# Identity products between the first loads, a new order table, and final sums shared between VectorE and GpSimd in a two-layer state-space and convolution kernel

## The chip, the cores and the metric

One core of one Trainium2 chip. The metric is the device time of one execution in microseconds; lower is better. Times are medians of several runs, with lowest and highest. All runs of this case are in the ordinary ("fast") state.

## The reference, cut to what matters

```python
x = x + A(layernorm(x), ...)   # state recurrence over 2048 steps, 640 channels, complex B, C, Lambda
x = x + B(layernorm(x), ...)   # long convolution by FFT: kv = shift(k) * v; y = irfft(rfft(kv) * rfft(ssm_k)); q * y
x = x + A(layernorm(x), ...)
x = x + B(layernorm(x), ...)   # same weights in both rounds; output bfloat16, 1 x 2048 x 640
```

B's convolution does not depend on `x`, so the kernel makes all of it (transforms as products with cosine and sine tables) in the first part, beside the loads, and only multiplies by it later. The last step, called B2 below, is `out = x + layernorm(x) * Y`, where Y is B's factor.

## The kernel before

Every piece of work is a task with a list of engines, an estimated length and the buffers it uses. A small list scheduler in the kernel's source places all tasks at build time; a table `WHEN` gives each task its rank. The instructions are then emitted in the order of the planned starts, and on the chip each engine takes its own in that order. So a number in `WHEN` decides who stands behind whom, on every engine.

```python
WHEN = {"warm": ..., "yt_ph0": ..., "kv_mm0:0": ..., "a_p0": ..., ...}     # cut: one rank for each task

def e_warm(_):                                   # first thing on TensorE: 72 products of the identity, to raise the clock
    for i in range(72):
        nc.tensor.matmul(s_warm.get()[:, P*(i%4):P*(i%4+1)], lhsT=ident_bf, rhs=ident_bf, start=True, stop=True)

# k-v product of one block: TensorE into one of four PSUM buffers, VectorE empties it (kv_ev)
def e_ev(_, h=h, s_pk=s_pk, s_vT=s_vT):
    nc.vector.tensor_tensor(s_vT.get()[:, sl], s_pk.get()[:], s_vT.get()[:, sl], ALU.mult)

def b_chunk(...):                                # B2: chunks 0 to 2 in one group of 4 quarters, chunk 3 in 4 groups of one
    for qs in groups:
        ... # statistics of the rows, cut
        if len(qs) == 1:                         # each quarter of chunk 3: two fused VectorE instructions
            scalar_tensor_tensor(b, x, nmean, Y, add, mult)          # e_u
            scalar_tensor_tensor(Y, b, rstd, x, mult, add)           # e_m
        else:                                    # whole chunk: normalise on ScalarE or VectorE, one product, four sums
            ln_apply(...)                                            # e_u, 4 times
            nc.vector.tensor_tensor(b, b, Y, ALU.mult)               # e_mm, 2560 columns
            nc.vector.tensor_tensor(Y, b, x, ALU.add)                # e_m, 4 times
```

Of the kernel before, what the change touches and what calls it, by code (L numbers as in the profile page):

```python
# [17 lines left out]
P = 128  # L18
# [34 lines left out]
    "warm": -5, "yt_io0": 2.55, "yt_ph0": 4.27, "yt_sin0": 5.89, "yt_neg0": 9.88, "yt_io6": 132.6, "yt_ph6": 8.2, "yt_sin6": 9.91, "yt_neg6": 13.01,  # L53
    "yt_io12": 8.8, "yt_ph12": 11.54, "yt_sin12": 13.59, "yt_neg12": 16.53, "yt_Ci": 21.14, "yt_Si": 22.8, "yt_nsi": 30.27, "yt_f0": 1.22, "yt_f2": 6.07,
    "yt_f3": 8.4, "yt_f4": 9.65, "yt_h0": 0.07, "yt_h1": 0.97, "yt_h2": 5.13, "yt_h3": 9.63, "kv_dsl": 1.97, "kv_kd": 2.73, "kv_k0": 13.36, "kv_k1":
    14.32, "kv_k2": 14.97, "kv_d0": 5.67, "kv_d1": 6.57, "kv_d2": 10.23, "kv_ds0": 10.65, "kv_lk0": -0, "kv_lv0": 9.8, "kv_mm0:0": 12.25, "kv_ev0:0":
    15.4, "kv_mm0:1": 15.02, "kv_ev0:1": 17.2, "kv_st0": 21.1, "kv_ds1": 13.44, "kv_lk1": 12.55, "kv_lv1": 15, "kv_mm1:0": 21.79, "kv_ev1:0": 25.02,
    "kv_mm1:1": 20.06, "kv_ev1:1": 22.17, "kv_st1": 32.7, "kv_ds2": 18.01, "kv_lk2": 35.6, "kv_lv2": 40.3, "kv_mm2:0": 48.16, "kv_ev2:0": 52.03,
    "kv_mm2:1": 40.92, "kv_ev2:1": 50.79, "kv_st2": 54.8, "kv_ds3": 30.92, "kv_lk3": 47.3, "kv_lv3": 43.8, "kv_mm3:0": 54.17, "kv_ev3:0": 56.25,
    "kv_mm3:1": 57.88, "kv_ev3:1": 59.99, "kv_st3": 76.1, "kv_ds4": 55.32, "kv_lk4": 68.7, "kv_lv4": 72.6, "kv_mm4:0": 78.97, "kv_ev4:0": 81.57,  # L60
    "kv_mm4:1": 72.36, "kv_ev4:1": 77.61, "kv_st4": 85.5, "a_pl": 0.17, "a_p0": 11.24, "a_p1": 13.98, "a_p2": 14.63, "a_p3": 15.78, "a_p4": 18.43, "a_p5":
    20.56, "a_p6": 23.36, "a_lamd": 23.86, "a_f": 28.37, "a_dd": 16.07, "a_ldB0": 2.4, "a_ldB1": 7.4, "a_wl00:0": 34.4, "a_wl00:1": 31.5, "a_wc00:0":
    37.93, "a_wm00:0": 39.1, "a_wc00:1": 40.53, "a_wm00:1": 40.04, "a_wl01:0": 40.21, "a_wl01:1": 37.9, "a_wc01:0": 42.58, "a_wm01:0": 49.98, "a_wc01:1":
    51.1, "a_wm01:1": 53.25, "a_wl02:0": 46.1, "a_wl02:1": 42.6, "a_wc02:0": 48.69, "a_wm02:0": 54.03, "a_wc02:1": 55.37, "a_wm02:1": 58.88, "a_wl03:0":
    71.4, "a_wl03:1": 56.5, "a_wc03:0": 74.94, "a_wm03:0": 75.97, "a_wc03:1": 76.97, "a_wm03:1": 79.87, "a_wl04:0": 65.2, "a_wl04:1": 74.9, "a_wc04:0":
    78.59, "a_wm04:0": 80.65, "a_wc04:1": 81.65, "a_wm04:1": 82.89, "a_b00:0": 9.82, "a_b0e0:0": (10.51, 0), "a_b00:1": 8.06, "a_b0e0:1": (9.33, 3),
    "a_b00:2": 11.53, "a_b0e0:2": (13.01, 1.5), "a_b00:3": 10.63, "a_b0e0:3": (12.42, -1), "a_b00:4": 7.7, "a_b0e0:4": (8.75, 3), "a_b01:0": 49.89,
    "a_b0e1:0": (50.52, 3), "a_b01:1": 14.62, "a_b0e1:1": (17.28, 0.8), "a_b01:2": 23.8, "a_b0e1:2": (24.94, 3), "a_b01:3": 18.33, "a_b0e1:3": (19.59,
    -1), "a_b01:4": 23.52, "a_b0e1:4": (24.36, 1.5), "a_b10:0": 33.92, "a_b1e0:0": (35, 3), "a_b10:1": 32.55, "a_b1e0:1": (33.68, 0), "a_b10:2": 25.31,
    "a_b1e0:2": (26.42, -1), "a_b10:3": 29.77, "a_b1e0:3": (31.02, 0), "a_b10:4": 26.8, "a_b1e0:4": (28.17, 3), "a_b11:0": 42.65, "a_b1e1:0": (43.58, -1),  # L70
    "a_b11:1": 28.31, "a_b1e1:1": (29.65, -1), "a_b11:2": 34.63, "a_b1e1:2": (35.54, -1), "a_b11:3": 46.77, "a_b1e1:3": (48.11, 99), "a_b11:4": 30.56,
    "a_b1e1:4": (31.47, -1), "a_gm0": 84.5, "a_ge0": (87.86, -1), "a_gm1": 87.84, "a_ge1": 90.96, "a_gm2": 104.18, "a_ge2": (107.4, 0), "a_gm3": 98.47,
    "a_ge3": (115.43, 1.5), "a_gm4": 92.78, "a_ge4": 96.07, "a_wl10:0": 97.9, "a_wl10:1": 89.8, "a_wc10:0": 115.48, "a_wm10:0": 107.45, "a_wc10:1":
    111.58, "a_wm10:1": 112.92, "a_wl11:0": 101.84, "a_wl11:1": 103.04, "a_wc11:0": 106.68, "a_wm11:0": 109.36, "a_wc11:1": 121.12, "a_wm11:1": 122.95,
    "a_wl12:0": 116.24, "a_wl12:1": 117.44, "a_wc12:0": 121.91, "a_wm12:0": 132.45, "a_wc12:1": 135.94, "a_wm12:1": 138.06, "a_wl13:0": 131.59,
    "a_wl13:1": 130.39, "a_wc13:0": 137.56, "a_wm13:0": 138.85, "a_wc13:1": 139.99, "a_wm13:1": 141.05, "a_wl14:0": 144.12, "a_wl14:1": 142.92,
    "a_wc14:0": 148.92, "a_wm14:0": 150.68, "a_wc14:1": 153.82, "a_wm14:1": 157.45, "a_ti": 20.17, "a_ta": 22.96, "a_t0": 26.17, "a_t1": 122.82, "a_t2":
    131.25, "yq0_kl": 4.8, "yq0_ka": 15.17, "yq0_KA:m0": 16.75, "yq0_KA:e0": (18.76, -1), "yq0_KA:m1": 19.31, "yq0_KA:e1": 20.32, "yq0_KA:m2": 17.03,
    "yq0_KA:e2": (17.86, -1), "yq0_KA:m3": 18.61, "yq0_KA:e3": (19.66, 99), "yq0_KB:m0": 25.89, "yq0_KB:e0": (27.01, 99), "yq0_KB:m1": 27.38, "yq0_KB:e1":
    (28.75, 0.8), "yq0_KB:m2": 24.08, "yq0_KB:e2": (25.52, 1.5), "yq0_KB:m3": 28.87, "yq0_KB:e3": (30.31, 0), "yq0_KB:m4": 26.57, "yq0_KB:e4": 27.91,  # L80
    "yq0_vl": 26.3, "yq0_VA:m0": 31.92, "yq0_VA:e0": (32.55, 0), "yq0_VA:m1": 31.61, "yq0_VA:e1": (32.24, 6), "yq0_VA:m2": 32.27, "yq0_VA:e2": (33.15,
    0.8), "yq0_VA:m3": 33.47, "yq0_VA:e3": (34.1, 99), "yq0_VB:m0": 35.91, "yq0_VB:e0": 36.98, "yq0_VB:m1": 37.48, "yq0_VB:e1": (38.73, 99), "yq0_VB:m2":
    36.58, "yq0_VB:e2": (37.97, 0), "yq0_VB:m3": 38.79, "yq0_VB:e3": (41.58, 0), "yq0_VB:m4": 40.18, "yq0_VB:e4": (39.51, 1.5), "yq1_kl": 28.99, "yq1_ka":
    34.59, "yq1_KA:m0": 39.9, "yq1_KA:e0": (41.76, 1.5), "yq1_KA:m1": 35.29, "yq1_KA:e1": (35.98, 6), "yq1_KA:m2": 35.57, "yq1_KA:e2": 36.58, "yq1_KA:m3":
    38.6, "yq1_KA:e3": (39.71, 0.8), "yq1_KB:m0": 43.29, "yq1_KB:e0": (44.32, 3), "yq1_KB:m1": 45.76, "yq1_KB:e1": (47.02, 0), "yq1_KB:m2": 44.86,
    "yq1_KB:e2": 46.12, "yq1_KB:m3": 43.97, "yq1_KB:e3": 45.22, "yq1_KB:m4": 47.51, "yq1_KB:e4": 49.78, "yq0_pw": 42.46, "yq0_IB:m0": 52.34, "yq0_IB:e0":
    53.78, "yq0_IB:m1": 51.44, "yq0_IB:e1": (52.78, 99), "yq0_IB:m2": 50.27, "yq0_IB:e2": (51.82, 0), "yq0_IB:m3": 53.95, "yq0_IB:e3": (54.47, 3),
    "yq0_IB:m4": 53.05, "yq0_IB:e4": 54.88, "yq0_tt": 64.47, "yq1_vl": 49.69, "yq1_VA:m0": 56, "yq1_VA:e0": (56.63, -1), "yq1_VA:m1": 57.69, "yq1_VA:e1":
    (58.43, 3), "yq1_VA:m2": 56.43, "yq1_VA:e2": (57.53, 3), "yq1_VA:m3": 56.75, "yq1_VA:e3": (57.6, -1), "yq1_VB:m0": 59.7, "yq1_VB:e0": 60.79,
    "yq1_VB:m1": 61.49, "yq1_VB:e1": (62.75, 0.8), "yq1_VB:m2": 60.37, "yq1_VB:e2": (61.69, 0.8), "yq1_VB:m3": 62.39, "yq1_VB:e3": 63.65, "yq1_VB:m4":  # L90
    61.27, "yq1_VB:e4": (62.15, -1), "yq0_IA:m0": 65.54, "yq0_IA:e0": (66.37, 6), "yq0_IA:m1": 66.03, "yq0_IA:e1": (67.27, 0.8), "yq0_st": 69.05,
    "yq2_kl": 52.2, "yq2_ka": 58.65, "yq2_KA:m0": 64.22, "yq2_KA:e0": (65.38, -1), "yq2_KA:m1": 63.55, "yq2_KA:e1": (64.19, -1), "yq2_KA:m2": 64.8,
    "yq2_KA:e2": (65.43, -1), "yq2_KA:m3": 63.86, "yq2_KA:e3": (64.49, 6), "yq2_KB:m0": 68.05, "yq2_KB:e0": (69.33, 99), "yq2_KB:m1": 66.86, "yq2_KB:e1":
    (68.17, 1.5), "yq2_KB:m2": 68.73, "yq2_KB:e2": (70.23, 0.8), "yq2_KB:m3": 69.62, "yq2_KB:e3": (71.13, 1.5), "yq2_KB:m4": 67.83, "yq2_KB:e4": (69.07,
    1.5), "yq1_pw": 66.59, "yq1_IB:m0": 78.02, "yq1_IB:e0": (79.4, -1), "yq1_IB:m1": 74.47, "yq1_IB:e1": (75.77, 0), "yq1_IB:m2": 76.21, "yq1_IB:e2":
    (77.78, 0.8), "yq1_IB:m3": 77.12, "yq1_IB:e3": (78.82, -1), "yq1_IB:m4": 75.54, "yq1_IB:e4": (76.67, 3), "yq1_tt": 80.49, "yq2_vl": 64.11,
    "yq2_VA:m0": 74.09, "yq2_VA:e0": (74.72, 0), "yq2_VA:m1": 71.61, "yq2_VA:e1": 72.94, "yq2_VA:m2": 71.25, "yq2_VA:e2": (73.84, 3), "yq2_VA:m3": 70.96,
# [278 lines left out]
def c_tt(n, slow=False):  # L376
    return 0.065 + 0.00104 * n if slow else 0.1 + 0.00053 * n
# [500 lines left out]
def b_chunk(S, nc, R, small, c, lname, s_x, sums_in, x_ready, s_Y, y_ready, sums_out, out, groups):  # L878
# [11 lines left out]
    for qs in groups:  # L890
# [4 lines left out]
        for i, q in enumerate(qs):  # L895
# [11 lines left out]
            else:  # L907
# [6 lines left out]
                def e_mm(_):  # L914
                    b = s_b.get()
                    nc.vector.tensor_tensor(b, b, s_Y.get(), ALU.mult)
# [626 lines left out]
```

## Time and profile before

| | before |
|---|---|
| time, median of 3 runs | 358.36 us (358.2 to 359.07) |
| span of the profiled run | 356.8 us |
| TensorE's last product ends | 345.70 us |
| VectorE's last instruction ends | 353.60 us, 7.90 us later |
| intervals of half clock (from the throttle records, before the end) | one, 36.85 to 40.26 us |

Read it as two numbers that add up: where TensorE ends, and how long VectorE still works after that (called the tail below). Some 3 us of store and program end follow.

### The profile page before, as it was taken

To read this page: it belongs to the slowest core of one execution; us is meant where nothing else is said; L and a number is where in the kernel's file an instruction comes from. 1 tells how busy PE (TensorE), PEld (TensorE's weight loads), DVE (VectorE), ACT (ScalarE), POOL (GpSimd) and SP (SyncE) were. 2 spreads that over 40 slices of the span, in tenths; PEclk is the share of its full clock that TensorE was granted. 3 is DMA by queue.
4 is the path that set the end of the run, shared out by engine and by line. 5 is a ranking of instruction groups with operands and counts; after the bars stand their busy time and mean duration, and the time that the engine had idled before them with its cause. 6 is when DMAs were issued, how large, how long until landed. Compare 5 with 4: busy or idle time off the path is not lost.

```text
span 356.8 us, 8409 instructions
## 1 busy us (share of the span) xinstructions
PE 327.5 (92%) x3534; PEld 247.6 (69%) x3565; DVE 315.1 (88%) x479; ACT 256.4 (72%) x406; POOL 20.8 (6%) x51
## 2 busy tenths in 40 slices
PE   7686998989998997999999999999999999999970
PEld 7346876867686986986685677686866767755640
DVE  8799798798799797999999969979999679999896
ACT  3999798898799999943378599797256577306850
POOL 5841003000000000000000000000000000000000
PEclk9999899999999999999999999999999999999996
DMA  7999999999999982790226690605032022220141
GB/s 193 208 235 188 182 184 217 193 186 202 237 245 163 184 174 46 144 233 2 62 73 119 137 333 34 147 18 132 0 68 81 3 16 59 75 75 2 50 172 73
DMA packets 118712, 45.91 MB, mean 129 GB/s; under 512 B 111629, under 2 KB 112914, under 8 KB 118674
## 3 DMA queue, kind: packets, MB, share of 16 engines
q1 hardware_dynamic: 118528, 45.36, 59.9%
q8 instruction: 28, 0.46, 0.5%
q14 instruction: 10, 0.08, 0.1%
q10 hardware_dynamic: 146, 0.01, 0.0%
HBM read 17.38 MB, written 7.86 MB: 71 GB/s over the span
## 4 chain that ended last, share of the span: by engine, by line
PE 69%; ACT 10%; DVE 8%; DMA 7%; issue 3%; SPq 2%; DVEq 0%; ACTq 0%
PE ps L859 31%; PE ps L770 11%; PE ps L773 11%; ACT b L382 6%; PE ps L608 3%; PE ps L1163 3%; DMA b<-in_A_C_im_dram 2%; DMA b<-in_B_v_dram 2%; DVE b L1169 2%; PE ps L1313 2%; DMA b<-b 2%; PE ps L1314 1%; PE ps L1208 1%; SPq L536 1%; DMA b<-in_B_k_dram 1%
## 5 line engine op out<-in xcount | busy, mean ns | idle before, releaser
L382 ACT ACTIVATE b<-ps 128x1024 bf16<-128x1024 f32 (+3 forms) x125 | 109.6, 945 | 29.5 <-PE ps L773 25.5
L859 PEld LDWEIGHTS <-b 128*128 128x128 bf16 x880 | 67.7, 98 | 48.3
L859 PE MATMUL ps<-W,b 128*128 128x128 bf16 (+1 forms) x629 | 95.7, 298 | 0.6
L770 PE MATMUL ps<-b,BT 128*128 128x256 bf16 x400 | 56.8, 273 | 0.0
L773 PE MATMUL ps<-b,BT 128*128 128x256 bf16 x400 | 56.7, 273 | 0.0
L808 DVE TENSOR_TENSOR_SCAN b<-rtab,b 128x1290 bf16<-128x1290 f32 x16 | 44.7, 2833 | 0.3
L773 PEld LDWEIGHTS <-BT 128*128 128x128 bf16 x400 | 39.1, 98 | 4.5
L770 PEld LDWEIGHTS <-BT 128*128 128x128 bf16 x400 | 38.6, 98 | 4.4
L726 ACT ACTIVATE b<-b,nmr,rstd 128x640 bf16<-128x640 f32 (+1 forms) x43 | 37.0, 915 | 6.2 <-DVE nmr L693 6.2
L681 ACT ACTIVATE junk<-b,nmean 128x640 bf16<-128x640 f32 x48 | 39.7, 828 | 1.5
L1232 PE MATMUL ps<-b,b 128*128 128x128 bf16 x170 | 35.1, 219 | 1.2 <-ACT G L382 0.7
L1235 PE MATMUL ps<-b,b 128*128 128x128 bf16 x170 | 35.4, 219 | 0.0
L1237 PE MATMUL ps<-b,b 128*128 128x128 bf16 x150 | 32.8, 219 | 0.0
L1234 PE MATMUL ps<-b,b 128*128 128x128 bf16 x150 | 32.8, 219 | 0.0
L384 DVE CAST b<-ps 128x1024 bf16<-128x1024 f32 (+2 forms) x24 | 26.2, 1109 | 6.3 <-PE ps L1208 2.7
L867 ACT ACTIVATE b<-ps 128x640 f32<-128x640 f32 x16 | 11.1, 697 | 22.8 <-PE ps L859 22.8
L859 PE MATMUL ps<-G,b 128*128 128x128 bf16 (+1 forms) x152 | 26.5, 295 | 0.4
L1163 PE MATMUL ps<-b,fd 128*128 128x512 bf16 x73 | 18.6, 380 | 3.8 <-POOL fd L1141 2.0
L1313 PE MATMUL ps<-b,b 128*128 128x128 bf16 x160 | 19.4, 219 | 2.6 <-ACT b L382 2.1
L1314 PE MATMUL ps<-b,b 128*128 128x128 bf16 x160 | 19.2, 219 | 0.0
L552 ACT ACTIVATE b<-b,s_F 128x640 f32<-128x640 bf16 x20 | 17.2, 859 | 1.8 <-DVE W L556 1.4
L556 DVE SCALAR_TENSOR_TENSOR W<-b,s_F 128x640 bf16<-128x640 bf16 x20 | 17.4, 882 | 1.0 <-ACT b L552 0.7
(210 smaller groups left out, 560.3 us busy)
## 6 DMA issues: line engine op xcount, KB each, us to landing
b<-in_A_x_dram SPq DMA_DIRECT2D x8, 640.0 KB, 4.9
b<-ysd SPq DMA_DIRECT2D x8, 640.0 KB, 5.1
b<-in_B_ssm_k_dram SPq DMA_DIRECT2D x5, 512.0 KB, 8.6
kvd<-b SPq DMA_DIRECT2D x5, 512.0 KB, 4.3
b<-kvd SPq DMA_DIRECT2D x5, 512.0 KB, 5.4
ysd<-b SPq DMA_DIRECT2D x5, 512.0 KB, 5.0
out_dram<-b SPq DMA_DIRECT2D x8, 320.0 KB, 2.2
tab<-in_A_B_re_dram SPq DMA_DIRECT2D x1, 800.0 KB, 7.4
```

The lines of the kernel that those rows point to most:

```text
L382: nc.scalar.activation(out, in_, ACT.Copy)
L681: nc.scalar.activation(small.junk, src(q), ACT.Square, bias=st["nmean"][:, i:i + 1], scale=1.0, accum_out=st["ssq"][:, i:i + 1])
L726: nc.scalar.activation(dst, src, ACT.Identity, bias=st["nmr"][:, i:i + 1], scale=st["rstd"][:, i:i + 1])
L770: nc.tensor.matmul(pb[:, jj, c2, :], lhsT=aw["BT1"][:, c2, j, k, :], rhs=uT[:, 0:2, k, :], start=(k == 0), stop=False)
L773: nc.tensor.matmul(pb[:, jj, c2, :], lhsT=aw["BT0"][:, c2, k, j * P:(j + 1) * P], rhs=uT[:, 2:4, k, :], start=False, stop=(k == NJ - 1))
L808: nc.vector.tensor_tensor_scan(gv, rt, gv, 0.0, ALU.mult, ALU.add)
L859: nc.tensor.matmul(pc[:, o0:o1], lhsT=lh, rhs=rh, start=(n == 0), stop=(n == len(ops) - 1))
L1163: nc.tensor.matmul(pk[:, 512 * b:512 * (b + 1)], lhsT=s_ds.get()[:, l, :], rhs=kT[:, t0:t0 + 512], start=(l == 0), stop=(l == 3))
L1232: nc.tensor.matmul(ps[:, g, 0, :], lhsT=T["Cf"].get()[:, q, :], rhs=are, start=True, stop=single)
L1234: nc.tensor.matmul(ps[:, g, 0, :], lhsT=T["Sf"].get()[:, q, :], rhs=A[:, 2 * q + 1, :], start=False, stop=True)
L1235: nc.tensor.matmul(ps[:, g, 1, :], lhsT=T["NSf"].get()[:, q, :], rhs=are, start=True, stop=single)
L1237: nc.tensor.matmul(ps[:, g, 1, :], lhsT=T["Cf"].get()[:, q, :], rhs=A[:, 2 * q + 1, :], start=False, stop=True)
```

## The change

Its intent: keep TensorE's clock up while it waits for the first loads and tables; take four of the last sums off VectorE, which works alone at the end; and find a better order for all of it.

```diff
 WHEN = {
-    "warm": -5, "yt_io0": 2.55, ...          # the whole table is made anew (cut)
+    ..., "fill0": 36.29, "fill1": 2.75, ...
 }
@@ b_chunk
-            if len(qs) == 1:
+            if qs[0] == 3:                     # only the last quarter keeps the two fused instructions
...
-                    b = s_b.get()
-                    nc.vector.tensor_tensor(b, b, s_Y.get(), ALU.mult)
+                    b = s_b.get()[:, qs[0]:qs[-1] + 1, :]
+                    nc.vector.tensor_tensor(b, b, s_Y.get()[:, qs[0]:qs[-1] + 1, :], ALU.mult)
...
-                            nc.vector.tensor_tensor(s_Y.get()[:, q, :], b, x, ALU.add)
+                            (nc.gpsimd if eng == "pool" else nc.vector).tensor_tensor(s_Y.get()[:, q, :], b, x, ALU.add)
+                    engs, ests = (("dve", "pool"), (0.77, 1.4)) if out is not None and c >= NCH - 2 else ...   # cut
@@ finish: one store for each quarter in chunk 3 (cut)
@@ before S.run()
+    for i, nm in enumerate(("kv_d0", "yt_ph0", "yt_sin0", "yt_ph6", "kv_d2", "yt_ph12", "yt_sin6", "yt_neg0", "yt_sin12", "kv_ev0:0")):
+        s_f = R_ps.new()
+        def e_fill(_, s_f=s_f):
+            for i in range(12):
+                nc.tensor.matmul(s_f.get()[:, P * (i % 4):P * (i % 4 + 1)], lhsT=consts["ident_bf"][:], rhs=consts["ident_bf"][:], start=True, stop=True)
+        S.add(f"fill{i}", "pe", 0.67, [tn[nm]], e_fill, uses=[s_f])
```

## The prediction

> **What bounds the kernel now.** I read the page first (busy shares and the 40 slices), then three long windows, then the chain that ended last, then short windows in the first 45 us, and last the timeline of VectorE and GpSimd.
>
> The page, then the table of windows (columns: TensorE, weight loads, VectorE, ScalarE, GpSimd busy us, granted clock, DMA share, GB/s):
> ```profile
> PE 327.5 (92%) x3534; PEld 247.6 (69%) x3565; DVE 315.1 (88%) x479; ACT 256.4 (72%) x406; POOL 20.8 (6%) x51
> 140.00:345.70 205.70, 204.60 (x1837) 148.08 (x1854) 188.73 (x246) 130.52 (x240) 0.00 (x0) 1.00 0.34 85
> 345.70:356.80 11.10, 0.00 (x1) 0.00 (x0) 7.79 (x13) 1.42 (x4) 0.00 (x0) 0.73 0.30 118
> 1.80:140.00 138.20, 122.93 (x1701) 99.52 (x1713) 117.86 (x214) 124.47 (x164) 19.60 (x43) 0.99 1.03 196
> ```
> There are three stages. From 140 to 345.7 us TensorE is busy 204.6 of 205.7 us: it is the bound, and no product is removed. From 1.8 to 140 us nothing is the bound alone: TensorE has 15.3 us of holes (138.2 - 122.9), ScalarE is busy 124.5, VectorE 117.9, and the DMA share is 1.03. After TensorE's last product at 345.7 come 11.1 us in which VectorE works alone. The chain in the last stage:
> ```profile
> 345.89 0.82 DVE b L871 x2
> 346.72 0.81 DVE b L901
> 347.55 0.89 DVE b L905
> 348.43 2.40 DVE b L901 x3
> 350.86 1.68 DVE b L905 x2
> ...
> 352.80 0.80 DVEq L1538
> ```
> L871 takes TensorE's last result; eight fused vector instructions (L901 and L905, one pair for each 128-row quarter of the last chunk) follow one after the other, and VectorE's last ends at 353.6 us. The store and the end of the program fill the rest, 3.2 us.
>
> In the early stage one thing concerns the added products, the clock (columns as above):
> ```profile
> 34.00:36.00 2.00, 0.31 (x11) 0.22 (x7) 2.00 (x7) 1.15 (x2) 0.00 (x0) 1.00 1.21 217
> 36.00:38.00 2.00, 2.00 (x32) 1.62 (x27) 1.79 (x3) 1.68 (x2) 0.00 (x0) 0.71 0.86 233
> 38.00:40.00 2.00, 2.00 (x27) 1.80 (x27) 0.34 (x1) 1.07 (x2) 0.00 (x0) 0.50 1.16 102
> ```
> After a hole of 1.7 us the granted clock drops to a half. Products there are 0.11 us apart on the chain instead of 0.06. Elsewhere from 8 us on the clock is 1.00. The first matmuls are slow too (22 and 21 in the 2 us windows from 2 and 4 us, 36 in that from 6 us), though the clock column says 1.00: it shows no throttle before the first recorded event.
>
> **What the Trainium skill says.** "TensorE: Matmul & The Clock Gate", section "Part 1: The HAM clock gate", says that the array runs at half clock until a window of about 3.4 us has been busy, and again after an idle one. The trace agrees: fast from about 6 us, and one slow interval of about 3.4 us (0.29 x 2 us + 0.50 x 2 us + 0.06 x 2 us in the next window = 1.7 us lost, which at half clock is 3.4 us). "SBUF — State Buffer", section "Who interferes with whom", says that a VectorE instruction with two SBUF inputs and a GpSimd instruction that reads SBUF exclude each other: the second waits until the first has ended. "GPSIMD Engine Reference", section 3.1, gives 4497 ns for a two-input add of 2048 columns on GpSimd, 2.2 ns a column. The trace of before agrees with the lock (start, length, engine, line):
> ```profile
> 24.64 0.16 DVE L479 TENSOR_TENSOR s_lam<-s_r,s_cs 128x5 f32<-128x5 f32 x1
> 24.71 0.37 DVE L480 TENSOR_TENSOR s_lam<-s_r,s_sn 128x5 f32<-128x5 f32 x1
> 25.48 2.31 DVE L487 TENSOR_TENSOR b<-ident_bf,s_lam 128x1920 bf16<-128x1920 bf16 x1
> L1141 POOL TENSOR_TENSOR fd<-ident_bf,skf x20: 392/394/2311, 12.5 to 55.7; 128x128 bf16<-128x128 bf16 x20
> ```
> A GpSimd product of 128 columns takes 394 ns, but the one that falls beside L487 takes 2311 ns, exactly L487's length. And L480, the same size as L479, takes 0.37 instead of 0.16 us beside a GpSimd product that had started.
>
> **The change, part by part.**
>
> 1. Ten tasks of twelve 128x128 products of the identity, placed by the build in TensorE's order from right after the 72 warm-up products to the first kernel transforms. 120 x 56 ns (36 in 2 us, warm) = 6.7 us of work. The holes from 8 to 28 us, in the 2 us windows, are 1.05 + 0.46 + 1.61 + 0.28 + 0.82 + 0.71 + 1.26 = 6.2 us, so nearly all of it fits where TensorE waits for loads and tables. The clock never dropped in that stretch, so they save nothing there. The one slow interval comes at 37 us, beyond nearly all of them. It costs some 20 products x 0.05 us + 12 products of L1208 at 0.9 instead of 0.6 us = 1.3 us on the chain. The new order may or may not have a hole there; I give it one half: -0.6 us.
>
> 2. The new order table. The build shows the same instructions interleaved otherwise: the two B loads now go ahead of the first k transpose, the phase tables come first on VectorE. Between 140 us and the end TensorE has 1.1 us of holes to win in all. In the first 140 us a better order could win part of 15.3 us, but the loads (1.03 DMA share, 196 GB/s) and ScalarE (90% busy) hold it. I put -0.5 us, with 2.5 us either way as the largest uncertainty.
>
> 3. The final sums. Of the last eleven instructions of this kind the build gives four to GpSimd: two of chunk 2 and those of quarters 0 and 1 of chunk 3. Quarters 0 to 2 of chunk 3 change from two fused VectorE instructions (0.81 + 0.89) to a normalisation on ScalarE, a product (0.50 us, from 1.49 us at 2560 columns and 1.29 at 2176) and a sum (0.82). The order of products on TensorE in the last four tasks is as before, so its last product should be ready at the same place. If both engines ran freely, VectorE from 345.9 would do L871 0.8, a pair of small ones 0.35, two products 0.9, L901 0.85, small ones 0.35, L905 0.85, then a product and a sum 1.3: end 351.3, a gain of 2.3 us. But a sum has two SBUF inputs on either engine. A GpSimd sum of 640 columns is, by the skill's rate, 640 x 2.2 = 1.4 us of reading (128 columns take 394 ns here). Walking it with the lock, from the chunk-2 product's end at 344.0 (L871 at 341.66, then 1.5 us): VectorE sum to 344.8, GpSimd to 346.2, VectorE to 347.0, GpSimd to 348.4, a small two-input instruction, L871 from 348.5 to 349.4 (before: 346.7), two products to 350.7, GpSimd to 352.1, L901 to 352.95, GpSimd to 354.35, L905, product, sum to 356.5. That is 2.9 us later than 353.6. If VectorE always goes first the two add up to 344.0 + 5.7 (its eight two-input instructions: 3 x 0.82 + 3 x 0.50 + 0.85 + 0.88) + 4 x 1.5 (1.4 and 0.1 to start) = 355.7, 2.1 us later. Between these I take +2.0, as some of it will overlap. One store for each quarter moves half as much after the last sum: gain at most 0.1 or 0.2 us, left out.
>
> Sum: 358.4 - 0.6 - 0.5 + 2.0 = 359.3 us.
>
> **Rivals.** (a) The tail is a gain: the lock is weaker for these shapes, or the sums on GpSimd fall beside instructions with one SBUF input (L871 reads PSUM). Then -2.3 instead of +2.0, and 355 us; for it speaks that L1169, with one input in PSUM, is never slowed beside GpSimd (1209 to 1225 ns). Against it: eight of VectorE's instructions there have two SBUF inputs. (b) The added products delay real ones, because TensorE takes them in order and each waits for a table on VectorE or ScalarE. For it: the 120 exceed the holes by 0.5 us, and a late table holds everything behind it. Against: the stage is held by loads, with 15 us of holes. It would make 361 to 363 us. (c) The new order and an unbroken clock win several us in the first 140 us, and the bound stage starts earlier: 352 to 355 us. The kernel is tuned and the DMA engines are full, so I give this less.
>
> **Range and chances.** The tail ranges from -2.3 to +2.9, the early part from -4 to +2.5. Together 355.8 to 362.5 holds it 8 times in 10. Two per cent is 7.2 us: faster needs (a) and a large (c) together, 0.04; slower needs (b) and the whole lock, 0.04.
>
> **What would show it.** In the changed profile: sums on GpSimd near 344 to 355 us with lengths over 1.5 us and VectorE's sums or products beside them stretched by as much; VectorE's last instruction 9 to 11 us after TensorE's last product instead of 7.9; the 120 products before 30 us at about 56 ns; TensorE saturated from 140 us plus or minus 2, its last product within 2 us of 345.7; the clock at a half in one 3.4 us window or none. It is wrong if GpSimd's sums run unstretched beside VectorE's, or if TensorE's last product moves by over 3 us.

## The result and the profile after

Ratios are the mean time of one kernel's fast runs over the mean of the other's in the same rounds, so they are not quite the ratio of the medians quoted.

The changed kernel takes 362.12 us (361.96 to 363.92, 4 runs) against 358.72 (358.2 to 359.47): ratio 1.0105, 95% interval 1.0067 to 1.0142. It is about 1% slower, within the 2% that counts as the same, and inside the predicted range.

| us | before | after |
|---|---|---|
| span of the profiled run | 356.8 | 360.5 |
| TensorE's last product ends | 345.70 | 347.85 |
| tail (VectorE's end minus that) | 7.90 | 9.65 |
| intervals of half clock before the end | one, 3.41 us | none after 8.23 us |

So 2.15 us come ahead of TensorE's end and 1.75 in the tail; the store and program end are 0.25 us shorter, which leaves the 3.7 us of the span.

The page of the changed kernel (busy us), then its table of windows (columns as in the prediction):

```profile
PE 334.5 (93%) x3685; PEld 253.8 (70%) x3685; DVE 316.6 (88%) x477; ACT 256.7 (71%) x407; POOL 25.6 (7%) x55
```
```profile
140.00:347.85 207.85, 206.12 (x1862) 148.45 (x1859) 188.43 (x243) 132.23 (x243) 1.66 (x1) 1.00 0.34 84
347.85:360.50 12.65, 0.00 (x1) 0.00 (x0) 9.33 (x15) 3.15 (x6) 5.74 (x4) 0.70 0.27 104
2.31:140.00 137.69, 128.40 (x1827) 105.37 (x1827) 117.71 (x216) 121.27 (x159) 16.55 (x43) 1.00 1.02 197
```

TensorE is saturated as before, at full clock throughout, but only after a last hole at 141.7 to 143.2 us (in the kernel before, the last holes lie at 134 to 138 us). It ends 2 us later: the early part is worse, not better. In the last stretch GpSimd appears with 5.74 us.

The timelines of VectorE and of GpSimd at the end (start, length, engine, line, operation; "x2" is two instructions of a kind in a row; the bracket gives idle time before and what ended it):

```profile
344.57 1.49 DVE L926 TENSOR_TENSOR b<-b,b 128x2560 bf16<-128x2560 bf16 x1
346.09 2.77 DVE L934 TENSOR_TENSOR b<-b,b 128x640 bf16<-128x640 bf16 x2
...
348.97 1.17 DVE L696 TENSOR_TENSOR nmr<-nmean,rstd 128x1 f32<-128x1 f32 x1
...
350.99 0.16 DVE L696 TENSOR_TENSOR nmr<-nmean,rstd 128x1 f32<-128x1 f32 x1
351.07 0.89 DVE L926 TENSOR_TENSOR b<-b,b 128x640 bf16<-128x640 bf16 x2
351.87 2.02 DVE L911 SCALAR_TENSOR_TENSOR b<-b,nmean,b 128x640 bf16<-128x640 f32 x1
...
354.00 1.17 DVE L696 TENSOR_TENSOR nmr<-nmean,rstd 128x1 f32<-128x1 f32 x1
```
```profile
346.19 3.93 POOL L934 TENSOR_TENSOR b<-b,b 128x640 bf16<-128x640 bf16 x2 [281.42 <-DVE b L926]
351.69 3.47 POOL L934 TENSOR_TENSOR b<-b,b 128x640 bf16<-128x640 bf16 x2 [1.56 <-ACT nmean L679]
```

While GpSimd adds, four VectorE instructions are stretched: one of the two sums (the pair takes 2.77 instead of 1.56 us, +1.21), a 128x1 product twice (1.17 instead of 0.16, +1.01 each) and L911 (2.02 instead of 0.81, +1.21). That is 4.4 us lost on VectorE, for four sums of 0.82 us taken off it.

In the early part, the chain that ended last shows in the changed kernel a small load at its head, and the timelines of VectorE show the four evacuations of the first two k-v blocks (L1169 before, L1180 after). Before:

```profile
17.19 1.23 DVE L1169 TENSOR_TENSOR b<-ps,b 128x1024 bf16<-128x1024 f32 x1 [0.35 <-DMA b<-in_B_v_dram]
18.64 1.21 DVE L1169 TENSOR_TENSOR b<-ps,b 128x1024 bf16<-128x1024 f32 x1
23.50 1.23 DVE L1169 TENSOR_TENSOR b<-ps,b 128x1024 bf16<-128x1024 f32 x1 [0.60 <-PE ps L1163]
27.71 1.21 DVE L1169 TENSOR_TENSOR b<-ps,b 128x1024 bf16<-128x1024 f32 x1
```

After:

```profile
7.88 0.21 DVE L448 CAST b<-b 20x128 f32<-20x128 bf16 x1 [2.29 <-DMA b<-in_A_Dskip_dram]
...
21.63 1.21 DVE L1180 TENSOR_TENSOR b<-ps,b 128x1024 bf16<-128x1024 f32 x1
23.90 1.21 DVE L1180 TENSOR_TENSOR b<-ps,b 128x1024 bf16<-128x1024 f32 x1
32.08 1.22 DVE L1180 TENSOR_TENSOR b<-ps,b 128x1024 bf16<-128x1024 f32 x1
35.49 1.22 DVE L1180 TENSOR_TENSOR b<-ps,b 128x1024 bf16<-128x1024 f32 x1
```

They come 4.4, 5.3, 8.6 and 7.8 us later. VectorE stands idle 2.29 us for a cast of the small parameters (task a_p0); and the last two evacuations stand behind two tables that the new order put ahead of them (a_f, L499 to L528, 28.30 to 32.1 us; a_t0, L641 and L642, 33.21 to 35.5).

### The profile page after: what moved, and what is told of

It is laid out like the page before. It is cut to its first block, busy times and chain, and to the rows that moved or that the text cites. A ratio compares the mean times of both kernels' runs of the same rounds, so it can differ in the third digit from the quotient of the medians.

```text
span 360.5 us, 8700 instructions
## 1 busy us (share of the span) xinstructions
PE 334.5 (93%) x3685; PEld 253.8 (70%) x3685; DVE 316.6 (88%) x477; ACT 256.7 (71%) x407; POOL 25.6 (7%) x55
## 4 chain that ended last, share of the span: by engine, by line
PE 63%; ACT 14%; DVE 13%; DMA 6%; issue 3%; ACTq 0%; DVEq 0%
PE ps L862 31%; PE ps L773 11%; PE ps L776 11%; ACT b L385 8%; PE ps L611 3%; DMA b<-b 2%; DVE b L1180 2%; DMA b<-in_B_v_dram 2%; DMA b<-in_A_Dskip_dram 2%; ACT BT L385 1%; PE ps L1324 1%; ACT b L555 1%; DVE b L934 1%; PE ps L1325 1%; PE ps L1219 1%
## 5 line engine op out<-in xcount | busy, mean ns | idle before, releaser
L385 ACT ACTIVATE b<-ps 128x1024 bf16<-128x1024 f32 (+3 forms) x127 | 110.9, 939 | 33.4 <-PE ps L776 27.6
L729 ACT ACTIVATE b<-b,nmr,rstd 128x640 bf16<-128x640 f32 (+1 forms) x42 | 35.9, 912 | 8.5 <-DVE nmr L696 7.9
L1246 PE MATMUL ps<-b,b 128*128 128x128 bf16 x170 | 35.5, 219 | 0.0
L387 DVE CAST b<-ps 128x1024 bf16<-128x1024 f32 (+1 forms) x22 | 24.2, 1112 | 6.6 <-PE ps L1248 5.2
L934 POOL TENSOR_TENSOR b<-b,b 128x640 bf16<-128x640 bf16 x4 | 7.4, 1868 | 283.0 <-DVE b L926 281.4
L862 PE MATMUL ps<-G,b 128*128 128x512 bf16 (+1 forms) x160 | 27.0, 299 | 0.0
```

Source lines behind the costliest of these rows:

```text
L385: nc.scalar.activation(out, in_, ACT.Copy)
L387: nc.vector.tensor_copy(out, in_)
L729: nc.scalar.activation(dst, src, ACT.Identity, bias=st["nmr"][:, i:i + 1], scale=st["rstd"][:, i:i + 1])
L862: nc.tensor.matmul(pc[:, o0:o1], lhsT=lh, rhs=rh, start=(n == 0), stop=(n == len(ops) - 1))
L1246: nc.tensor.matmul(ps[:, g, 1, :], lhsT=T["NSf"].get()[:, q, :], rhs=are, start=True, stop=single)
```

## The experiments

Three theories were put: the lock (sums on GpSimd shut out VectorE's two-input instructions), the clock (the added products do keep the clock up and are worth something), and the order (the new order costs the early part; which step of it?). Every kernel gave the reference's result unless it is said. In after_fill0, after_poolwrite and the last group the changed kernel's order is kept, so that only the edit differs. Twelve runs were made, on three chips, so times of different groups are compared by their ratios to the kernel before. "Ends" in the tables below is TensorE's last product in the profiled run. Seven of them:

| run | time (us) | before, same rounds | ratio [95%] | ends | tail |
|---|---|---|---|---|---|
| after_fill0 | 364.54 (363.69 to 365.69) | 358.62 | 1.0165 [1.0144, 1.0186] | 350.14 | 9.66 |
| table_only | 363.6 (363.21 to 364.1) | 358.62 | 1.0140 [1.0121, 1.0158] | 348.73 | 9.58 |
| after_oldtail | 363.31 (362.25 to 364.4) | 358.62 | 1.0132 [1.0109, 1.0155] | 347.75 | 9.59 |
| tail_only | 360.79 (358.57 to 362.65) | 358.62 | 1.0062 [1.0031, 1.0094] | 346.24 | 9.40 |
| tail_only_nopool | 357.97 (357.64 to 358.26) | 358.37 | 0.9991 [0.9975, 1.0007] | 345.24 | 7.80 |
| before_fills | 358.88 (357.64 to 360.07) | 358.37 | 1.0017 [0.9990, 1.0043] | 344.86 | 7.90 |
| after_poolwrite (wrong on purpose) | 361.97 (359.04 to 362.77) | 358.37 | 1.0089 [1.0052, 1.0125] | 351.41 | 5.34 |

### The changed kernel without its added products (after_fill0)

```diff
-            for i in range(12):
+            for i in range(0):          # in e_fill; all orders kept
```

> The changed kernel with every instruction in its place, but the ten added tasks emit no product (the 120 identity products are gone, nothing else moves). Theory A (the added products fit in holes and are harmless; the 2 us by which TensorE ends later come from the new order, in which VectorE stands 2.29 us before a small cast that waits for the last of the little parameter loads): time within 0.5 us of the changed kernel's 362.1, TensorE's last product again near 347.8. Theory B (the added products delay real ones, rival b of the prediction): 360 or less, TensorE's last product back at 346 or earlier. Theory C (they keep the clock up and so are worth something): slower than 362.1 by 1 us or more, with a window at half clock in the first 45 us.

Measured: 364.54 us, ratio 1.0165 against the changed kernel's 1.0105. Its table of windows (clock is the third figure from the right):

```profile
10.00:12.00 2.00, 0.22 (x2) 0.23 (x3) 1.86 (x8) 0.74 (x2) 0.00 (x0) 0.89 1.02 225
12.00:14.00 2.00, 1.60 (x14) 1.41 (x14) 1.83 (x7) 0.01 (x1) 0.00 (x0) 0.50 1.13 238
14.00:16.00 2.00, 0.00 (x0) 0.00 (x0) 1.97 (x5) 1.43 (x3) 1.45 (x2) 0.50 0.95 89
16.00:18.00 2.00, 1.09 (x6) 0.63 (x6) 1.97 (x8) 1.95 (x3) 1.81 (x5) 0.50 1.19 240
```

The changed kernel's granted clock is 1.00 in each of these windows. Without the added products it is a half from 11.58 to 21.82 us, real products run slowly from 16 us on, and the time is longer: theory C holds. TensorE ends at 350.14 instead of 347.85 us, but not all of these 2.29 us comes from the missing products. This profiled run has a second interval of half clock, from 144.70 to 148.11 us. We matched TensorE's products one by one in the two packed traces (the matched figures below are made in the same way): the changed kernel leads by 0.7 to 0.8 us from 90 to 144 us, and by 2.28 us only after that interval. The other four runs have a mean clock of .972 to .975 against its .968, so they seem to be without it.

So in this order the products hold the clock up, and they are worth 0.7 to 1.0 us of TensorE's end (the second figure is from the next section). That is no more than the scatter: in three traces whose order on TensorE is that of before, without added products, TensorE ends between 345.24 and 346.24 us.

### The new order and the added products, each without the other parts (table_only, after_oldtail)

```diff
 # table_only: the new order, the tail of before (b_chunk and the ranks of B2's chunks 2 and 3), products as range(0)
 # after_oldtail: the same with the 120 products
```

> The new order for everything but the last two chunks, no added products, the old tail. Theory A (the order alone costs 2 us in the first 140 us): 360.3 us, TensorE's last product near 347.8. Rival B (the added products cost them, the order is neutral): 358.7, last product near 345.7.

> The changed kernel with its added products and its order, but the last two chunks as in the kernel before (fused sums on VectorE, none on GpSimd, ranks of the old table for these tasks). Theory A (GpSimd's sums and VectorE's two-input instructions shut each other out, which costs 1.7 to 2 us at the end): 360.2 us, VectorE's last instruction 7.9 us after TensorE's last product instead of 9.65. Rival (the tail costs nothing, all of the loss is in the early part): 362.

Measured: ratios 1.0140 and 1.0132. The new order alone loses about 5 us (2 were expected, so theory A is right in direction and too small). 3.0 of them are ahead of TensorE's end in the profile (348.73 against 345.70). The expectation for after_oldtail failed: the tail of before did not bring its 7.9 us with it, but 9.59. In the new order VectorE does chunk 2's product (1.49 us) only after the last but one evacuation of TensorE's results: at 344.73 us behind that at 343.71 in after_oldtail, at 344.57 behind 343.82 in the changed kernel. Before, it stood ahead of it, at 340.08 against 341.66. From that evacuation on VectorE has next to no idle time (0.19 us in the changed kernel), so what stands behind it lengthens the tail by its own length. The tail belongs to the order as well as to the form of the last chunk, and the parts do not simply add. The added products show 1.0 us here in the profile and only 0.3 us in the medians.

### The new tail alone, with and without GpSimd (tail_only, tail_only_nopool)

```diff
 # before, with b_chunk of the changed kernel and its ranks for B2's chunks 2 and 3; TensorE's order is that of before
-  engs, ests = (("dve", "pool"), (0.77, 1.4)) if out is not None and c >= NCH - 2 else ("dve", ...)   # tail_only
+  engs, ests = "dve", ...                                                                             # tail_only_nopool
```

> The kernel before with the new treatment of the last two chunks alone (normalisation on ScalarE, sums shared with GpSimd, new ranks for these tasks). TensorE's order is that of before, so its last product should stay near 345.7. Theory A (the lock): 360.5 us, 1.8 us over before, with sums and small instructions on VectorE stretched by 1.0 to 1.2 us each. Rival (the tail gains, and the loss is elsewhere): 356.5.

> The kernel before with the new treatment of the last two chunks, but all sums on VectorE, none on GpSimd. Theory A (the lock): without it VectorE's walk from its last-but-one TensorE result is 11.8 us instead of 13.4, so its last instruction comes 7.7 us after TensorE's last product (9.4 with GpSimd) and the time is 1.7 us under the 360.8 of the same tail with GpSimd: 359.1. Rival (not the lock but the later chunk product and the chain over ScalarE make the tail long): within 0.5 us of 360.8.

Measured: 360.79 (1.0062) with GpSimd, 357.97 (0.9991) without. VectorE's timeline without GpSimd:

```profile
343.48 2.30 DVE L1673 TENSOR_TENSOR b<-b,b 128x640 bf16<-128x640 bf16 x3
...
345.88 0.16 DVE L1435 TENSOR_TENSOR nmr<-nmean,rstd 128x1 f32<-128x1 f32 x1
...
349.24 0.88 DVE L1650 SCALAR_TENSOR_TENSOR b<-b,nmean,b 128x640 bf16<-128x640 f32 x1
```

All the stretching is gone (three sums in 2.30, 0.16, 0.88), VectorE does four sums more, and its tail is 1.6 us shorter. The difference of the two ratios, 0.7% or 2.5 us, is larger than this 1.6, and than expected. In the profiles the rest is TensorE's end, 1.0 us apart although its order is the same in both; that cannot be put down to the sums.

The new form without GpSimd has the same tail as before (7.80 against 7.90) for two reasons that cancel. It saves VectorE about 1.5 us (three quarters at a product of 0.45 and a sum of 0.77 in place of 0.81 and 0.89), but chunk 2's product now stands behind the last but one evacuation here too, which costs 1.49. With the product ahead of it, the tail would be some 6.3 us: an estimate from these rows, which no run has tried.

### GpSimd that only writes (after_poolwrite)

```diff
-  nc.gpsimd.tensor_tensor(s_Y.get()[:, q, :], b, x, ALU.add)
+  for _ in range(3): nc.gpsimd.memset(s_Y.get()[:, q, :], 0.0)      # wrong on purpose: half of the rows of two chunks are zero
```

> The changed kernel with a wrong result on purpose: GpSimd's four sums are replaced by three memsets each of the same rows, which read nothing from SBUF. All waits and the order stay. Theory A (it is the reading that shuts VectorE out): VectorE's sum is 0.82 us again instead of 2.03, L911 0.81 instead of 2.02, the small two-input ones 0.16 instead of 1.17, and the time falls by some 3 us to 359. Rival (waits between the engines stretch them): they stay long, 362.

GpSimd's timeline, then VectorE's beside it:

```profile
349.72 7.87 POOL L1685 MEMSET b<- 128x640 bf16 x12 [283.05 <-DVE b L1675]
```
```profile
349.64 1.56 DVE L1687 TENSOR_TENSOR b<-b,b 128x640 bf16<-128x640 bf16 x2
...
351.31 0.16 DVE L1445 TENSOR_TENSOR nmr<-nmean,rstd 128x1 f32<-128x1 f32 x1
...
353.27 0.88 DVE L1660 SCALAR_TENSOR_TENSOR b<-b,nmean,b 128x640 bf16<-128x640 f32 x1
```

GpSimd is busy for the whole of it, longer than in the changed kernel (7.87 against 7.4 us), and VectorE is not stretched at all: the tail is 5.34 us, 2.56 shorter than before. So it is the reading of SBUF by GpSimd that shuts VectorE out, not its being busy. 5.34 us is what the change hoped for. (The time itself, 361.97, missed the 359 expected and is no gain, because TensorE ended at 351.41 in that run, with intervals of half clock at 33.5 and 146.1 us.)

### Added products in the order of before (before_fills)

```diff
+ FILL = {"kv_d1": 12, "a_b00:4": 18, "kv_mm0:0": 24, "a_b10:2": 20}   # 74 identity products, in the PSUM buffer of the task they stand before
```

> The kernel before, every instruction in its place, with 74 identity products added in its early holes (12 behind the warm-up, 18 before the first B transposes, 24 before the first k-v products, 20 before the second B products), each in the slot of the task that follows. Theory C (added products keep the clock up): 0.5 to 1.5 us faster than before where runs of before fall to half clock in the first 30 us; the window at 37 us stays. Theory A (no value): 358.6 within 0.4 us. Theory B (they delay real work): over 359.5.

Measured: 1.0017, unclear. The profile shows no half clock at all and TensorE's end 0.84 us earlier, but the six runs have two peaks (357.6 to 358.2 and 359.6 to 360.1), and the mean granted clock, .987 to .989 for five of them, does not tell the peaks apart. A gain is not shown here.

### Which step of the new order costs the early part (after_p0late, after_evfirst, after_early, after_early_nopool)

```diff
 # on the changed kernel, between sorting the order and emitting it
+ swap a_p0 and yt_h1                            # after_p0late: the cast that waits for the small load goes behind its neighbour
+ move a_f and a_t0 behind kv_ev1:1              # after_evfirst: tables behind the evacuations
+ both                                           # after_early
+ both, and all sums on VectorE                  # after_early_nopool
```

> The changed kernel with two neighbouring tasks of VectorE swapped: the cast of the little parameters (it waits 2.29 us for a load that lands at 7.75 us) behind the small table instead of in front of it. Theory A (this wait, in front of everything that VectorE does for the tables, costs the early stage): the wait is gone, the first k-v evacuation comes near 19.5 us instead of 21.6, TensorE ends 1.5 to 2 us earlier (346), time 360.3. Rival (the early stage is held elsewhere, by loads and ScalarE): 362 within 0.5 us.

> The changed kernel with two tasks of VectorE, the table of a_f (L499 to L528, 3.8 us) and a_t0 (2.3 us), moved behind the two evacuations of the second k-v product (kv_ev1:0 and kv_ev1:1, L1180); every other order is kept. Theory E (the new order loses the early part because these tables stand before the evacuations, so that two of the four PSUM buffers stay held and TensorE waits for them at 33 us and after): the waits of fill8 and fill9 for L1180 (0.69 and 0.83 us) go, TensorE's last product comes 1.5 to 2 us earlier than 347.85, about 346, and the time is 360.3 us, ratio to before 1.004. Rival F (the early part is held by loads and tables that arrive when they arrive, so that a wait removed comes back a few us later, as it did in the run with the late parameter load): last product 347.3 to 348.5, time 361.8, ratio 1.009. A third way: the tables come too late now for the transforms that need them, and the time is over 363.

> The changed kernel with both early repairs (the swap of a_p0 and yt_h1, the two tables behind the two evacuations) and GpSimd's four sums kept. It stands between two runs made: the changed kernel with one of the repairs (361.7 and 362.8 us), and both repairs with all sums on VectorE (358.1 us, end of VectorE 8.06 us after TensorE's last product). If the two repairs act only together and the sums on GpSimd cost 1.6 us: tail 9.6 to 9.7 us, last product 345.4 (347.1 if one late half-clock window falls into it), time 359.3 to 359.7 us without such a window, ratio to before 1.004. If the repairs bring nothing even together and all of the gain came from the sums: 361.5 to 362, ratio 1.009. If the sums cost nothing here: 358.1, ratio 1.000.

> The changed kernel with three repairs together: the swap of the two neighbours a_p0 and yt_h1 on VectorE, the two tables behind the two evacuations, and all final sums on VectorE (none on GpSimd). Theory E with the lock: TensorE's last product at 345.5 to 346, VectorE's end 9.6 us or less after it (four sums of 0.82 more on VectorE, 3.3 us, against 4.4 us of stretching less: about 8.6), time 358.8, ratio 1.001. Rival F: last product 347.3 to 348.5, time 361, ratio 1.007. If the tail is no shorter than 9.6 us without GpSimd, the lock is not what makes the tail long in this order.

| run | time (us) | before, same rounds | ratio [95%] | ends | tail |
|---|---|---|---|---|---|
| after_p0late | 361.7 (359.57 to 363.06) | 358.37 | 1.0082 [1.0055, 1.0109] | 348.62 | 9.65 |
| after_evfirst | 362.83 (361.18 to 364.85) | 358.83 | 1.0122 [1.0084, 1.0160] | 349.64 | 9.66 |
| after_early | 361.91 (361.0 to 362.88) | 358.39 | 1.0091 [1.0055, 1.0127] | 346.93 | 9.66 |
| after_early_nopool | 358.08 (357.55 to 360.21) | 358.83 | 0.9995 [0.9963, 1.0027] | 347.07 | 8.06 |

Each repair by itself failed to bring the time expected. TensorE's timeline of the changed kernel, of the run without the added products, and of after_p0late, at the same place, then two windows of after_p0late (clock is the third figure from the right):

```profile
33.35 0.83 PE L1530 MATMUL ps<-ident_bf 128*128 128x128 bf16 x12 [2.29 <-DVE b L1180]
```
```profile
34.05 0.22 PE L1339 MATMUL ps<-b,W 128*128 128x128 bf16 x1 [2.41 <-DVE b L1929]
```
```profile
31.54 0.83 PE L2282 MATMUL ps<-ident_bf 128*128 128x128 bf16 x12 [2.29 <-DVE b L1932]
```
```profile
32.00:34.00 2.00, 2.00 (x27) 2.00 (x25) 1.97 (x3) 0.76 (x2) 0.00 (x0) 0.63 1.45 193
34.00:36.00 2.00, 2.00 (x22) 2.00 (x20) 1.53 (x2) 1.06 (x3) 0.00 (x0) 0.51 1.44 157
```

L1180, L1929 and L1932 are the same evacuation in the three sources. In the changed kernel TensorE waits 2.29 us from 31 us on for a PSUM buffer that the late evacuation frees. Without the added products a real product waits 2.41 us at the same place, so those products are not its cause.

In after_p0late the same wait stands there, as long but 1.81 us earlier. By matched products this run leads the changed kernel by 1.81 us before and after the wait. The lead falls to 0.18 us between 32.3 and 36.1 us, inside an interval of half clock (32.54 to 35.95 us) that the changed kernel does not have. So that interval took the gain back, and not the wait; the expectation for after_evfirst ("as it did in the run with the late parameter load") had read this wrongly.

With the two tables moved, the wait is gone, with the swap and without it. after_evfirst leads the changed kernel by 2.70 us at 33 us. It loses 1.6 of them at a wait of 1.56 us for VectorE (to 37.72 us), 1.3 around a wait of 1.95 us for a load (b<-kvd, to 82.85 us), and 1.56 in an interval of half clock at 144 us. With both repairs the lead is 4.26 us at 33 us and some 2.5 us from 70 to 143 us. That is more than the 2.15 us by which the changed kernel's TensorE ends later than before. So in the traces these two steps of the new order carry the cost of the early part, and what each brings by itself (1.8 us until its interval, 1.1 us until the load) nearly adds up.

The intervals themselves follow a pattern that the throttle records show. In each of the 14 traces the clock changes only at whole multiples of 3.41 us from the first record, and this grid begins elsewhere in each run. Ahead of TensorE's end there are 1374 stretches of the grid at full clock. In 20 of them TensorE is busy for 52% or less; after 15 of these 20 the next stretch is at half clock, and after none of the others. So it matters how the grid cuts a hole, and that differs from run to run. The wait at 29 to 31.5 us in after_p0late lies whole in one stretch (33% busy, then half clock), while in the changed kernel an edge at 32.12 us cuts it in two. The last hole, at 138 to 144 us, leaves 48% in one stretch in after_early (half clock follows) and 54% in the changed kernel (none). Why 5 of the 20 were spared is not shown.

In the time little of all this shows. after_early's tail came as expected, and so did TensorE's end when its late interval is counted. Its 361.91 us, ratio 1.0091, did not: that is the figure written for "the repairs bring nothing even together". Its throttle records have one interval of half clock at 141.65 us and those of after_evfirst one at 144.11; the changed kernel's have none. TensorE is the bound there, and by matched products such an interval costs 1.56 us. Runs of one kernel part by it: after_evfirst's three runs with a mean granted clock of .986 to .989 took 361.2 to 361.7 us, those with .981 and .982 took 364.0 to 364.9. (One interval of 3.41 us at half clock is 1.7 / 358 = .005 of the mean. The mean also holds the half clock after TensorE's end, 5.9 to 10.3 us in these traces, so it tells the runs apart only roughly.) At 346.93 with one such interval, less 1.56, after_early would end at 345.4, as before; that is an estimate, and the times do not bear it out. The one run with a mean of .986, which should be without the interval, took 361.0 us, where 359.3 to 359.7 was expected. So what the two repairs are worth in time is not shown. The run that could show it, all sums on VectorE without the repairs, was not made.

Taking the sums off GpSimd brings 3.8 us in the medians of after_early and after_early_nopool (two chips; 3.4 us by the ratios), 1.6 of them in the tail of the profile (9.66 against 8.06, TensorE's end 0.14 apart). Part of the rest is again the interval: four of the six runs without GpSimd have a mean clock of .988 or more, one of the six with it .986 and the others .982 or less. At equal clock (.983 and .984 without, .981 and .982 with) it is 359.9 and 360.2 against 361.25 to 362.45, about 1.7 us; at .988 or more without and .986 with, it is 357.55 to 358.28 against the one run of 361.0, about 3 us. Whether the sums bear on how often the interval falls cannot be said with six runs each.

### The two parts of the change that did not lose, in the order of before (before_fills_tail)

```diff
 # tail_only_nopool with the 74 products of before_fills
```

> The kernel before with the two parts that did not lose by themselves: 74 identity products in the holes of the first 40 us, and the new form of the last chunk's tail with all its sums on VectorE. If the two add: 344.9 + 7.8 us in the profile, so 355.6 to 355.9 for the span and 357.6 for the time, ratio 0.998. If the products bring nothing (the run with them alone was two-peaked, 357.7 and 360): 358.0, ratio 0.999, or 1.001 with the upper peak. Faster than before by over 2% is expected by no theory.

Measured: 357.64 us (357.13 to 359.28) against 358.83, ratio 0.9984 [0.9957, 1.0011]: as expected, and not shown to be faster than before. No version was found that clearly beats the kernel before.

## Why the prediction was right or wrong, point by point

- **The time.** 359.3 was predicted, 362.12 measured: right (no change by over 2%) and near the upper end of the range. The estimate itself missed by 2.8 us, nearly all of it in step 2; the 2.5 us either way allowed for the early part covered it.
- **Step 3, the tail.** Right in mechanism. "+2.0" against 1.75 in the profile. The walk that the prediction made had each GpSimd sum hold VectorE for 1.4 us; the trace shows 1.0 to 1.2 us lost for each of four, two of them on a 128x1 product, "a small two-input instruction" to which the walk gave no price of its own. The walk put chunk 2's product behind the evacuation at 341.66. That is where the changed kernel has it (344.57 behind 343.82), but the trace of before has it ahead, at 340.08, so 1.49 us of the loss that the walk found come from the order and not from the lock; the prediction did not part the two. Rival (a), no lock, is refuted by after_poolwrite: 5.34 us, its "-2.3" as -2.56, appears only when GpSimd does not read. What was not foreseen is that the new order makes the tail of before as long (9.59): the place of that product is worth as much as the lock.
- **Step 1, the added products.** The step "The clock never dropped in that stretch, so they save nothing there" failed. It was read in the old order, where no interval of half clock lies between 8 and 28 us. In the new order there are larger holes there, and without the products the clock is a half for 10.2 us. They are worth 0.7 to 1.0 us of TensorE's end in the profiles, with after_fill0's late interval left out (0.3 to 2.1 us by the ratios). That the 0.6 is about right in size is luck: it stood for the interval at 37 us, which the new order does not have even without the products.
- **Step 2, the order.** The step "I put -0.5 us" has the wrong sign: the new order without the products ends TensorE 3.0 us later in table_only (348.73 against 345.70), and 4.4 us later in after_fill0, of which its late interval is 1.5. Both lie beyond the 2.5 us either way that was allowed. The step's ground, that the loads and ScalarE hold the early part whatever the order, is what failed: by the traces a cast that VectorE waits for, and two tables ahead of two evacuations, make up the loss (2.5 us, after_early). Against -0.5 and -0.6, the errors of steps 2 and 1 are +3.5 and -0.4 by the one pair of runs, +3.4 and -0.1 by the other without the late interval. The 3.1 to 3.3 that remain, less 0.25 for the tail and rounding, are the 2.8 us that the prediction missed by.
- **Rival (b)** ("the added products delay real ones") gave the right size, 361 to 363 us, for a wrong reason. A group of them does wait 2.3 us, but for a PSUM buffer, and a real product waits as long without them. **Rival (c)**, a gain early, did not come.
- **What would show it.** GpSimd's sums of 1.5 to 2.0 us, VectorE's end 9.65 us after TensorE's, no half clock: as stated. TensorE's last product "within 2 us of 345.7" was missed by 0.15 us, one group of the 120 products ran after 30 us (at 33.35), and TensorE had holes until 143 us instead of 142.

## What to carry to other kernels

Before moving work to an engine that shuts the loaded one out, as GpSimd did VectorE here, price what the loaded engine loses in each instruction beside it, also the smallest: here four sums of 0.82 us saved cost 4.4 us. An order that looks free of waits on the engine that is moved can hold a PSUM buffer and stop another engine 10 us later; look for who waits for the task behind. When a repair seems to bring nothing, match the instructions of the two traces before calling it undone: here an interval of half clock, and not another wait, had taken 1.6 us back. Products that only keep the clock up are worth what the holes of that very order would cost, so measure them with the order they come with.

## What the Trainium skill lacked or had wrong

- "TensorE: Matmul & The Clock Gate", section "Part 1: The HAM clock gate": it speaks of an idle window, and does not say how busy a window must be to keep or win back the clock. Here a hole of 1.7 us was enough for one half-clock interval of 3.41 us (before, 36.85 us): no stretch busier than 52% was followed by half clock, and 15 of the 20 at or below that were. The clock came back after stretches that were 80% to 100% busy. In after_fill0 it stayed at a half for 10.2 us although TensorE was busy 1.60 of 2 us (12 to 14 us) and 1.09 of 2 us (16 to 18 us). Its free-running window agrees with the traces: the clock changes on a grid of 3.41 us whose first record lies anywhere from 4.96 to 8.35 us after the start.
- "SBUF — State Buffer", section "Who interferes with whom": agrees, also that a GpSimd instruction that only writes does not interfere (12 memsets over 7.87 us, VectorE's sums 1.56 a pair). What it lacks is a figure for how long a two-input VectorE instruction waits: a 128x1 VectorE product that takes 0.16 us alone took 1.17 us.
- "GPSIMD Engine Reference", section 3.1: its rate gives 1.4 us for a sum of 640 columns, an estimate from that page; the runs show 1.98 us for three of four beside VectorE and 1.53 for the fourth. No run has such a sum alone.
- No page read here says that the clock column of a profile shows 1.00 until the first throttle record: the first products ran 22 in 2 us, slow, beside a clock of 1.00.
